# Linear attention into a gated long convolution: k and v dealt to 116 partitions in runs of five tokens, and the last output rows of two batches computed as one tile

## The chip, the cores and the metric

The kernel runs on one core of one Trainium2 chip. The metric is the device time of one execution in microseconds; the number given for a kernel is the median of its runs. A core has a matrix engine (TensorE, PE in the profile; its weight loads are PEld), a vector engine (VectorE, DVE), a scalar engine (ScalarE, ACT), GpSimd (POOL) and a queue engine (SyncE, SP). Each runs its own instructions in order and waits on semaphores. Transfers are issued from SP, ACT and POOL and carried by the core's 16 DMA engines.

## What is computed

Inputs are q, k and v of shape (8 batches, 8 heads, 576 tokens, 64), and three weights. First comes a linear attention, in which phi weights the positive part of a row by cosine and sine of its token's place:

```python
def phi(x, c, s):
    r = np.maximum(x, 0.0)
    return np.concatenate([r * c, r * s], axis=-1)
kv  = einsum('bhsf,bhsd->bhfd', phi(k), v)      # sum over the tokens s
z   = sum over s of phi(k)
att = einsum('bhsf,bhfd->bhsd', phi(q), kv) / (phi(q) . z + 1e-6)
```

The heads side by side make x of shape (8, 576, 512). Then x @ w_proj gives three blocks x1, x2, x3; x2 is convolved along the tokens with a filter, by a Fourier transform of length 576; and the output is (x1 * conv(x2) * x3) @ w_out, of shape (8, 576, 512) in float32.

What matters for the change: the sum over tokens in kv and z does not care which token lies on which partition, so long as k and v agree and the cosine and sine columns fit. The rows of q, and so of the output, do have fixed places.

## The kernel before

**Tokens on partitions.** A batch has 576 = 5 * 115 + 1 tokens. `load_rows` (L156) puts tokens 0 to 511 of four or eight heads on 128 partitions, four successive tokens each (one transfer, runs of 256 elements), and tokens 512 to 575 on partitions 0 to 63 as a fifth column of 64 elements (a second transfer). The unused half of the fifth column, partitions 64 to 127, is filled with zeros by memsets (`step_pad` L234, and L246 for `k32` and `v32`). q, k and v all have this layout. The token numbers are in `s4_i` (L207), from which ACT makes the cosine column `ccol` and the sine column `scol` (L248 and L251); `tcol` and `epsc` come from these.

**Who loads.** The first half of batch 0's k and v comes from SP into the float32 tiles `k32` and `v32` (`step_load32`, words `Sk`, `Sv`). Everything else comes from POOL into six float16 buffers (`step_load`, words `Lq`, `Lk`, `Lv`), cast on the way.

**The steps of a batch.** `pk` (L504 on) makes kp = relu(k) times cosine and sine, 20 instructions a batch on ACT or DVE, through `tsc` (L111) or directly (L514). `va` casts v beside a column of ones (L538, through `ev`, L134 and L138). `kv` (L557) is the sum over tokens: for each of 8 heads five matmuls of 65 columns over all 128 partitions. `pq` makes the products of q, `qt` transposes them (on PE in batches 0 and 1, by a DMA transpose from SP after), `num` multiplies with kv and divides into `att`. `fx` and `pr` go to x2, `dft`, `mul` and `inv` do the convolution, `xt` and `ga`/`gb` the two gates (L736), `g` and `y` their product, and `out` the last matmul.

**The last rows.** The output of a batch comes in four tiles of 128 rows (`out` groups 0 and 1, L824) and the last 64 rows (group 2). For these `y` writes the tile `ye` of 64 columns. `out_tile` (L818) then runs eight matmuls (L829): 64 rows by 256 columns each, the two halves of the 512 columns on the two halves of the PSUM partitions. `left` (L853) evicts 128 x 256 elements on ACT and stores them by two transfers of 64 rows.

**What sets the order.** The order on every engine is written out by hand: the string that `run` (L890) reads. A word such as `pk0.1'a*2` runs two parts of step `pk` of batch 0, half 1, on ACT (`'v` is DVE); each part ends at a `yield`. An engine takes its instructions in this order. PSUM tiles (`unit`, L69) come from a ring of four. Words with `~` are loads that also wait for the last DVE instruction and DMA transpose named before them (`hold`, L148).

Of the kernel before, what the change touches and what calls it, by code (L numbers as in the profile page):

```python
# [17 lines left out]
def kernel(  # L18
# [19 lines left out]
    nc = tc.nc  # L38
# [21 lines left out]
    NM = NC * 128  # L60

# [104 lines left out]

    def step_load(nm):
        def load(b, half):
            raw_t[(b, nm)] = raw_buf[(3 * b + "qkv".index(nm)) % len(raw_buf)]
            load_rows(nc.gpsimd, raw_t[(b, nm)], {"q": q, "k": k, "v": v}[nm], b, at(half))  # L170
            yield
        return load

    def step_load32(nm):
        def load(b, half):
            load_rows(nc.sync, k32 if nm == "k" else v32, k if nm == "k" else v, b, at(half))
            yield
        return load
# [26 lines left out]
    def step_iota(part):  # L205
        if part == 0:
            iota("s4_i", [128, NJ], lambda t: [  # L207
                (t[:, 0:4], [[1, 4]], 0, 4), (t[0:64, 4:5], [[1, 1]], NM, 1),
                (t[64:128, 4:5], [[1, 1]], 0, 1),
            ])  # L210
            yield
            return
# [29 lines left out]
    def step_cols():  # L242
        nc.vector.memset(warm, 0.0)
        nc.vector.memset(half_pi, PI / 2.0)
        for r in (k32, v32):
            nc.vector.memset(r[64:128, :, 4 * D : 5 * D], 0.0)  # L246
        yield
        nc.scalar.activation(  # L248
            out=ccol, in_=cc["s4_i"], func=AF.Sin, scale=-(PI / 2.0) / S, bias=half_pi
        )  # L250
        nc.scalar.activation(out=scol, in_=cc["s4_i"], func=AF.Sin, scale=(PI / 2.0) / S)  # L251
        yield
# [5 lines left out]
        nc.vector.reciprocal(out=epsc, in_=ccol)  # L258
        yield
        nc.vector.tensor_tensor(out=tcol, in0=epsc, in1=scol, op=AL.mult)  # L260
# [244 lines left out]
    def step_pk(b, half):  # L505
# [4 lines left out]
        for j in range(NJ):  # L510
            for x, col in enumerate((ccol, scol)):
                dst, src, c = kp_t[b][:, j, hs, x], rw[:, hs, ds(j * D, D)], col[:, j : j + 1]
                if which[0] == "a":
                    nc.scalar.activation(out=dst, in_=src, func=AF.Relu, scale=c)  # L514
                else:
                    tsc(dst, src, c, AL.mult, 0.0, AL.max)
                yield
# [21 lines left out]
    def step_va(b, x):  # L539
# [3 lines left out]
            va_buf[b % 2][:, hs, :, 0:D],  # L543
            (v32 if b == 0 and x < 2 else raw_t[(b, "v")])[:, hs].rearrange(
# [11 lines left out]
    def step_kv(b, half):  # L556
# [3 lines left out]
        for g in range(hv.start, hv.stop):  # L560
            for h in range(4 * g, 4 * g + 4):
                for j in range(NJ):
                    nc.tensor.matmul(  # L563
                        u[:, g, ds((h % 4) * 65, 65)], kp[:, j, h].rearrange("p a b -> p (a b)"),
                        va[:, h, j, 0:65], start=(j == 0), stop=(j == NJ - 1),
# [220 lines left out]
    def step_y(b, c, n):  # L786
# [24 lines left out]
        if "ye" not in moe[b]:  # L811
            moe[b]["ye"] = late["p"].tile([128, NC, 64], FP16, tag="ye", bufs=2, name=f"ye{b}")
        tt(
            out=moe[b]["ye"][:, c : c + n].rearrange("p c (a t) -> p c a t", t=4),
# [5 lines left out]
    def out_tile(b, t, dst, cs):  # L820
        y = moe[b]["y"]
        for c in cs:
            if t < 4:
# [3 lines left out]
                continue  # L827
            for hf in range(2):
                nc.tensor.matmul(  # L829
                    dst[ds(64 * hf, 64), 0 : DM // 2], moe[b]["ye"][:, c],  # L830
# [22 lines left out]
    def left(b, u):  # L853
        os_ = late["p"].tile([128, DM // 2], FP32, tag="os4", bufs=1, name=f"os{b}_4")
# [35 lines left out]
    def run(plan, **batch):  # L890
# [15 lines left out]
        cols io0 pad1 Sk0.0 pad2 cols io2 rows io1 cols rows th tf warm0.12 cols*5 Sv0.0  # L906
        rows pad0 th'v rows*3 th'v cols*3 rows pk0.0'a*2 rows pk0.0'a*2 tf pk0.0 rows
        pk0.0'a tf pk0.0 cols*2 rows va0.1 cols ones0 rows*2 pk0.0*2 rows va0.0'v pk0.0'a
        th'v Lq0.0 Lq0.1 kv0.0 rows pq0.0 pq0.0'a*4 pq0.0 pq0.1*2 qt0.1 pq0.1*3 Lk0.1 qt0.0
        pq0.1'a qt0.2 kv0.0 qt0.1'b num0.1 tf pk0.1'a pk0.1*3 tf pk0.1 qt0.0'c num0.0 pk0.1  # L910
        ones1 pk0.1'a pk0.1*2 Lv0.1 va0.2 num0.0 num0.1 pk0.1'a va0.3'v qt0.2'b Lw0 kv0.1*2
        num0.1 num0.0 num0.1 cols Lw2 num0.0 qt0.3 rows Lq1.2 num0.2*2 cols*2 xp0.0 qt0.3'b
        rows num0.2 rows num0.2 Lk1.2 xp0.0*2 xp0.0'a num0.3*4 xp0.1 Lv1.2 ga0.0 gb0.3 Lw1
        xp0.1*2 pad4 cols pad5 ti xp0.1'v cols pad3 Lf gb0.0*2 tf ga0.0 gb0.0 ga0.0 Lf
        gb0.3*2 ga0.3 gb0.2 ti tf th ~Lq2.2 cols ~Lk2.2 cols pq1.2*2 pq1.2'a pq1.2*2 pq1.2'a
        rows gb0.2 ga0.3 ga0.1*2 ga0.3'v ti cols fx0.1 fx0.0 pk1.2 gb0.2 pk1.2 gb0.1*2 ga0.1
        fx0.3 fx0.1 pk1.2*2 fx0.0'v ga0.2 pk1.2 fx0.2 th gb0.1 fx0.3 fx0.2 ga0.2*2 pk1.2
        tf'v pk1.2*4 qt1.0 va1.0'v kv1.2 va1.1'v kv1.2 th kv1.2 qt1.1 g0.0.2 qt1.0'v th
        ~Lq3.1 tf qt1.0'v qt1.1'v qt1.2 qt1.1'v qt1.2 ~Lk3.0 qt1.2 num1.0*3 tf pr0.1 th
        num1.1 num1.0 num1.2 g0.2.2 num1.1 tf ~Lq3.0 num1.2 num1.1 pr0.1 tf ti pr0.0 num1.2  # L920
        num1.1 qt1.3 num1.2 pr0.0 pr0.2 qt1.3 dft0.0 feo0 pr0.2 dft0.0 feo1 h0 qt1.3'v xp1.0
        ti xp1.0 pq2.2 fx1.1 pq2.2 h0'v h1 ~Lv2.2 pq2.2 xp1.0 pq2.2 pk2.2 xp1.0'v pk2.2
        pk2.2'a h0 fx1.1 pk2.2 num1.3*3 pq2.2 num1.3 pq2.2 qt2.3 h2 qt2.0 fx1.2 h1 pk2.2 h1
        pk2.2 xp1.1 fx1.3 xp1.1 ~Lk3.1 ~Lq4.1 ~Lv3.1 h2 fx1.2 xp1.1'v fx1.3 xp1.1'v fx1.0
        pk2.2*2 dft0.1 dft0.1'v ~Lo dft0.2 ga1.0 fx1.0 dft0.2 mul0 ti mul0 pr1.0 pr1.2 ti*2
        mul0 ga1.0 mul0 pr1.1 pr1.1'v pr1.0 ga1.0 inv0.1 inv0.0 ~Lq4.0 ti pk2.2 late pr1.2
        dft1.2 dft1.0 dft1.2'v inv0.1 dft1.1 pk2.2 inv0.0 inv0.2 va2.0'v dft1.0 kv2.2 pq3.2
        va2.1'v inv0.3 kv2.2 y0.0.2 ~Lk4.1 y0.0.2 dft1.1 inv0.2 ga1.2*2 mul1 gb1.2 mul1
        qt2.1 kv2.2 num2.0 ~Lv3.0 qt2.2 num2.0 inv0.3 num2.1 pq3.2'a ga1.2 gb1.2 ~Lv4.0
        num2.1 num2.0 num2.1 num2.0 num2.1 gb1.3*2 mul1*2 gb1.2 gb1.1*2 pq3.2'a pq3.2 gb1.3  # L930
        pq3.2'a ga1.1 pk3.2 gb1.1 num2.2 ~Lk4.0 num2.2*3 y0.0.2 ga1.1 y0.0.2 fx2.1 y0.2.2
        ga1.1 y0.2.2 gb1.0*2 pk3.2'a fx2.1 inv1.1 fx2.2 pk3.2 gb1.0 inv1.1 fx2.2 ga1.3
        y0.2.2 ga1.3 inv1.0 inv1.0'v ga1.3 xp2.0 num2.3*3 xp2.0*3 num2.3 pk3.2 inv1.3*2
        y0.0.2 inv1.2*2 fx2.0*2 fx2.3*2 g1.0.2 ga2.0 xp2.1*2 pr2.0 xp2.1*2 pq3.2 ga2.0
        y0.2.2 qt3.0 va3.0'v y1.0.2 pk3.2 pk3.2'a*2 pk3.2 y0.2.2 pk3.2'a pq4.2 pr2.1 ga2.0
        qt3.2 pq4.2 out0.0 pr2.2 pr2.1 pr2.0 out0.0 dft2.1 y1.0.2 dft2.0 ~Lq5.0 va3.1'v
        y1.0.2 ~Lq5.1 ~Lv4.1 y1.0.2 pk3.2 ~Lv5.0 qt3.1 y1.2.2*2 pr2.2'v dft2.1 y1.2.2 dft2.2
        kv3.2*2 y1.0.2 gb2.1 y0.2.2 gb2.1 dft2.0 g1.2.2 y0.0.2 pq4.2'a ~Lv5.1 qt3.3 dft2.2'v
        kv3.2 gb2.0*2 mul2*2 num3.0*4 ~Lk5.0 gb2.1 gb2.0 gb2.3 pk4.2'a gb2.3*2 ~Lk5.1 out0.2
        ga2.2*2 fx3.0 out0.2 pq4.2'a ga2.1 mul2*2 ga2.2 fx3.0 num3.1*2 num3.2*2 pk4.2'a  # L940
        ga2.1 num3.1 pk4.2 out0.1 num3.2 num3.1 y1.2.2 ga2.1 num3.2 num3.3*2 pk4.2 pk4.2'a
        num3.3*2 ga2.3 gb2.2 ga2.3 xt3 pq4.2'a gb2.2 out0.1 fx3.1 fx3.2 ga2.3 inv2.1 gb2.2
        fx3.3 pq4.2 qt4.0 qt4.1 pk4.2'a pk4.2*2 fx3.3 fx3.1'v fx3.2'v inv2.1 pk4.2'a inv2.0
        pk4.2 inv2.0 g2.2.2 qt4.2 va4.0'v va4.1'v y2.0.2*2 pr3.0*2 pr3.1 pq5.2 pr3.1 kv4.2
        g2.0.2 y1.2.2 ~Lk6.0 ~Lq6.0 kv4.2*2 pq5.2'a pr3.2 ga3.0 pk5.2 pr3.2'v pk5.2 y1.2.2
        ga3.0 inv2.2 out0.2 dft3.2 ~Lk6.1 inv2.2'v dft3.0*2 dft3.2'v dft3.1*2 num4.0 inv2.3
        pk5.2*2 inv2.3 num4.0 y1.0.2 pq5.2'a gb3.1 num4.1 num4.0*2 num4.2 mul3 gb3.1 num4.1
        ~Lq6.1 pq5.2'a out1.0*2 num4.2 num4.1 pq5.2'a qt4.3 num4.1 ga3.1*2 pq5.2'a y2.0.2
        num4.2 gb3.0 num4.2 y2.0.2 y2.2.2 num4.3 gb3.0 num4.3 out0.0 out1.1*2 y2.2.2 num4.3
        gb3.3 fx4.0 qt5.2 num4.3 fx4.2 gb3.2 mul3 xt4 gb3.3'v ga3.2 qt5.1 mul3 pk5.2 fx4.0  # L950
        fx4.2 mul3 fx4.1 g3.0.2 inv3.0 qt5.0 gb3.2 qt5.3 fx4.3 y2.2.2 ga3.2 fx4.1 pk5.2*3
        inv3.0'v fx4.3 pk5.2 inv3.1 inv3.1'v y2.2.2 y3.0.2*2 pk5.2'a pr4.0 y3.0.2 inv3.3
        pr4.0 y2.2.2 inv3.3 out1.2*2 pr4.2 out1.2 pr4.1 y3.0.2 ~Lq7.0 va5.0'v kv5.2 y2.0.2
        va5.1'v pr4.1'v inv3.2 pq6.2 pr4.2 kv5.2 ga4.0 pk6.2*2 ~Lv6.1 ga4.0'v inv3.2 kv5.2
        out0.1 dft4.2 pq6.2 pq6.2'a*2 pq6.2 dft4.1 dft4.0 ga3.3 dft4.2 dft4.0'v pk6.2 dft4.1
        mul4 ~Lq7.1 num5.0*3 ga3.3 ~Lv6.0 num5.0 ~Lk7.1 gb4.1 num5.1*2 g3.2.2 pk6.2'a*2
        out2.0 gb4.1 y3.2.2 out1.0 out2.0 pk6.2'a pk6.2 pk6.2'a gb4.0 num5.1 gb4.0 num5.1
# [61 lines left out]
```

## Time and profile before

| | us |
|---|---|
| median of 3 runs (222.70 to 224.93) | 223.49 |
| the profiled execution | 224.69 |
| its span | 222.9 |
| PE busy | 207.7 |
| DVE busy | 194.7 |
| ACT busy | 170.7 |
| POOL busy | 65.5 |

How to read what follows. Busy time is given per engine over the span; the chain of work is what ended last, followed backwards. A line of the timeline has start and length in us, engine, line of the kernel, operation, output tile <- input tiles, shape, and in brackets how long the engine had been idle and what ended that. A line of the groups has the count after the shape, then total busy time and mean ns of one, then idle time ahead of them. `SPq` is an issue on SP's queue: its length is the time of issuing, not of the transfer. Queue q0 carries what POOL issues, q1 what SP issues. The profile lists for the first loads from SP 3.9 us (k) and 5.9 us (v) from issue to landing, and medians of 6.9, 7.2 and 6.5 us for the half loads of q, k and v from POOL.

### The profile page before, as it was taken

To read this page: it belongs to the slowest core of one execution; us is meant where nothing else is said; L and a number is where in the kernel's file an instruction comes from. 1 tells how busy PE (TensorE), PEld (TensorE's weight loads), DVE (VectorE), ACT (ScalarE), POOL (GpSimd) and SP (SyncE) were. 2 spreads that over 40 slices of the span, in tenths; PEclk is the share of its full clock that TensorE was granted. 3 is DMA by queue.
4 is the path that set the end of the run, shared out by engine and by line. 5 is a ranking of instruction groups with operands and counts; after the bars stand their busy time and mean duration, and the time that the engine had idled before them with its cause. 6 is when DMAs were issued, how large, how long until landed. Compare 5 with 4: busy or idle time off the path is not lost.

```text
span 222.9 us, 5869 instructions
## 1 busy us (share of the span) xinstructions
PE 207.7 (93%) x2316; PEld 142.8 (64%) x2316; DVE 194.7 (87%) x473; ACT 170.7 (77%) x275; POOL 65.5 (29%) x105
## 2 busy tenths in 40 slices
PE   7388989999999999999999999799999999999990
PEld 2176776574888476756686667476876667477630
DVE  7998999989999989989999997889888797589930
ACT  4796989998898999888784975877787736476651
POOL 8892456213962096003500184002200000000000
PEclk9979999999999999999999999999999999999996
DMA  5999999999999999999999999997999940823084
GB/s 170 190 186 192 191 209 193 175 138 210 144 189 184 173 161 182 169 195 163 170 157 194 200 199 182 146 300 156 110 177 149 326 132 3 197 94 138 22 258 165
DMA packets 90907, 38.39 MB, mean 172 GB/s; under 512 B 58944, under 2 KB 86592, under 8 KB 90880
## 3 DMA queue, kind: packets, MB, share of 16 engines
q0 software_dynamic: 38944, 16.26, 59.8%
q1 hardware_dynamic: 51568, 21.17, 46.0%
q10 hardware_dynamic: 368, 0.59, 0.7%
q8 instruction: 18, 0.29, 0.5%
q14 instruction: 9, 0.07, 0.1%
HBM read 33.69 MB, written 9.44 MB: 193 GB/s over the span
## 4 chain that ended last, share of the span: by engine, by line
PE 67%; DVE 14%; DMA 10%; ACT 3%; issue 2%; POOL 2%; ACTq 0%; DVEq 0%; POOLq 0%
PE x L736 22%; PE x L680 11%; PE out L824 10%; DMA xt<-att 4%; PE kv L563 4%; PE num L606 4%; PE dft L711 3%; PE fx L634 3%; DMA out_dram<-os 3%; DMA raw<-in_q_dram 3%; PE inv L770 3%; PE inv L774 2%; DVE kp L111 2%; DVE yf L116 2%; DVE qp L111 2%
## 5 line engine op out<-in xcount | busy, mean ns | idle before, releaser
L736 PE MATMUL x<-xt,wp 128*128 128x288 f16 x512 | 71.2, 286 | 0.6 <-DMA xt<-att 0.3
L736 PEld LDWEIGHTS <-wp 128*128 128x128 f16 x512 | 47.9, 98 | 15.8 <-issue 2.8
L680 PE MATMUL x<-wp,fx 128*128 128x512 f16 (+1 forms) x160 | 34.6, 381 | 0.0
L824 PE MATMUL out<-wo,y 128*128 128x512 f16 x128 | 30.1, 379 | 0.0
L138 ACT ACTIVATE os<-out 128x1024 f32<-128x1024 f32 (+2 forms) x24 | 18.3, 767 | 12.5 <-PE out L824 10.1
L116 DVE TENSOR_TENSOR att<-num,rcp 128x640 f16<-128x640 f32 x32 | 26.0, 819 | 0.6
L680 PEld LDWEIGHTS <-fx 128*128 128x128 f16 (+1 forms) x160 | 13.6, 100 | 15.0 <-issue 2.1
L138 ACT CAST x0s<-x 128x576 f16<-128x576 f32 x27 | 17.2, 641 | 6.0 <-PE x L736 5.1
L138 ACT CAST x2s<-x 128x576 f16<-128x576 f32 x28 | 17.8, 639 | 4.8 <-PE x L736 4.7
L138 ACT ACTIVATE x2f<-x 128x1024 f16<-128x1024 f32 (+1 forms) x18 | 16.2, 903 | 6.6 <-PE x L680 5.6
L158 POOL DMA_DIRECT2D raw<-in_q_dram x14 | 11.2, 797 | 31.4 <-ACT x0s L138 18.2
L824 PEld LDWEIGHTS <-y 128*128 128x128 f16 x128 | 12.1, 98 | 12.6 <-issue 0.4
L138 ACT CAST fx<-fx 128x576 f16<-128x576 f32 x29 | 17.8, 648 | 1.8 <-PE fx L640 1.5
L138 ACT CAST eq<-inv 128x576 f16<-128x576 f32 x26 | 16.0, 648 | 3.9 <-PE inv L774 3.3
L158 POOL DMA_DIRECT2D raw<-in_k_dram x13 | 10.5, 811 | 27.0 <-DVE rcp L617 14.6
L770 PE MATMUL inv<-itab,yf 128*128 128x144 f16 x128 | 16.9, 226 | 1.2 <-ACT x2f L138 0.9
L158 POOL DMA_DIRECT2D raw<-in_v_dram x13 | 10.5, 805 | 21.8 <-DVE rcp L116 17.3
L774 PE MATMUL inv<-itl,yf 128*128 128x288 f16 x64 | 16.8, 286 | 0.0
L563 PE MATMUL kv<-va,kp 128*128 128x65 f16 x320 | 12.4, 193 | 4.0 <-DVE va L134 3.8
L563 PEld LDWEIGHTS <-kp 128*128 128x128 f16 x320 | 11.6, 98 | 5.8 <-ACT kp L514 4.0
L606 PEld LDWEIGHTS <-qpt 128*128 128x128 f16 x320 | 13.0, 98 | 3.6 <-issue 0.9
L606 PE MATMUL num<-kvs,qpt 128*128 128x65 f16 x320 | 14.3, 194 | 0.9 <-ACT qpt L138 0.5
(163 smaller groups left out, 432.8 us busy)
## 6 DMA issues: line engine op xcount, KB each, us to landing
out_dram<-os SPq DMA_DIRECT2D x30, 256.0 KB, 3.2
raw<-in_q_dram POOLq DMA_DIRECT2D x12, 256.0 KB, 6.9
raw<-in_k_dram POOLq DMA_DIRECT2D x11, 256.0 KB, 7.2
raw<-in_v_dram POOLq DMA_DIRECT2D x11, 256.0 KB, 6.5
wp<-in_moe_w_proj_dram POOLq DMA_DIRECT2D x3, 512.0 KB, 8.6
raw<-in_q_dram POOLq DMA_DIRECT2D x2, 512.0 KB, 12.1
raw<-in_k_dram POOLq DMA_DIRECT2D x2, 512.0 KB, 13.3
raw<-in_v_dram POOLq DMA_DIRECT2D x2, 512.0 KB, 10.5
```

Of the source, the lines that this page charges most:

```text
L111: last_dve[0] = nc.vector.tensor_scalar(out=out, in0=in0, scalar1=s1, scalar2=s2, op0=op0, **({"op1": op1} if op1 else {}))
L116: last_dve[0] = nc.vector.tensor_tensor(out=out, in0=in0, in1=in1, op=op)
L138: return nc.scalar.copy(out=out, in_=in_) if mul is None else nc.scalar.mul(out=out, in_=in_, mul=mul)
L158: first = queue.dma_start(out=rw[:, to, 0 : 4 * D], in_=src[b, hs, 0:NM].rearrange("h (p j) d -> p h (j d)", j=4),)
L563: nc.tensor.matmul(u[:, g, ds((h % 4) * 65, 65)], kp[:, j, h].rearrange("p a b -> p (a b)"), va[:, h, j, 0:65], start=(j == 0), stop=(j == ...
L606: nc.tensor.matmul(u[:, hh, ds(t * 65, 65)], qpt_buf[:, h, ds(t * 128, 128)], kvs[:, h // 4, ds((h % 4) * 65, 65)], start=True, stop=True,)
L634: nc.tensor.matmul(uf[:, ds(256 * t, 144)], att[:, c, t], fm.rearrange("p v a -> p (v a)"), start=(t % 2 == 0), stop=False,)
L680: nc.tensor.matmul(dst, fx[:, c, ds(128 * ch, n)], wp16[:, c, ds(DM, DM)], start=(c == cs[0]), stop=(c == cs[-1]),)
L736: nc.tensor.matmul(u[:, hf, 0:HS], wp16[:, i, ds(w * DM + c * 128, 128)], xt[:, i, ds(HS * hf, HS)], start=(i == 0), stop=(i == NC - 1),)
L770: nc.tensor.matmul(u[:, comp, ds(par * QS, QS)], yf[:, comp, ds(par * DM + c * 128, 128)], itab[:, par + 4 * comp], start=(par == 0), stop ...
L774: nc.tensor.matmul(u[:, comp, 0:HS], yf[:, comp, 2 * DM : NF], itl[:, c, comp].rearrange("p a b -> p (a b)"), start=False, stop=True,)
L824: nc.tensor.matmul(dst, y[:, c, ds(QS * t, 128)], wo16[:, c], start=(c == 0), stop=(c == NC - 1),)
```

## The change

k and v get a layout of their own. Partition p holds tokens 5p to 5p + 4, for p from 0 to 115; partition 115 has one valid token (575), its other four places hold what follows in memory, that is the next head's first tokens. One transfer with runs of 320 elements loads a half (four heads) or a whole batch. Only the very last half, at the end of the input, takes two: 115 partitions, and one token. The kv matmuls read 116 partitions for column 0 and 115 for columns 1 to 4, so the extra places never enter. `kp` and `va` are made on 116 partitions. The zero filling stays for q's buffers alone (`pad0`, `pad3`). `ccol` and `scol` now follow a new iota `k_i` with 5p + j; `tcol` and `epsc` are made from two further columns in the old order, `cq` and `sq`. q keeps `load_rows`.

For batches 0 to 5 the last 64 rows of two batches are computed together: `ye` holds both, four matmuls of 128 x 512 replace two times eight, one eviction of 128 x 512 replaces two of 128 x 256, and two stores of 64 rows x 512 replace four. Batches 6 and 7 stay as they were.

```diff
+    BP = B - 2
+    KP = S // NJ + 1
+    KJ = (KP,) + (KP - 1,) * (NJ - 1)
...
+    def load_runs(queue, rw, src, b, hs):
+        to = slice(0, rw.shape[1]) if rw.shape[1] < NH else hs
+        rows = src[b, hs].rearrange("h s d -> h (s d)")
+        last = b == B - 1 and hs.stop == NH
+        n = KP - 1 if last else KP
+        runs = bass.AP(
+            tensor=rows.tensor, offset=rows.offset, ap=((NJ * D, n), rows.ap[0], (1, NJ * D))
+        )
+        hold(queue.dma_start(out=rw[0:n, to], in_=runs))
+        if last:
+            queue.dma_start(
+                out=rw[n:KP, to, 0:D], in_=rows[:, (S - 1) * D :].unsqueeze(0)
+            )
...
-            load_rows(nc.gpsimd, raw_t[(b, nm)], {"q": q, "k": k, "v": v}[nm], b, at(half))
+            (load_rows if nm == "q" else load_runs)(nc.gpsimd, raw_t[(b, nm)], {"q": q, "k": k, "v": v}[nm], b, at(half))
...
-            load_rows(nc.sync, k32 if nm == "k" else v32, k if nm == "k" else v, b, at(half))
+            load_runs(nc.sync, k32 if nm == "k" else v32, k if nm == "k" else v, b, at(half))
...
+            iota("k_i", [128, NJ], lambda t: [(t, [[1, NJ]], 0, NJ)])
...
-        for r in (k32, v32):
-            nc.vector.memset(r[64:128, :, 4 * D : 5 * D], 0.0)
         yield
-        nc.scalar.activation(
-            out=ccol, in_=cc["s4_i"], func=AF.Sin, scale=-(PI / 2.0) / S, bias=half_pi
-        )
-        nc.scalar.activation(out=scol, in_=cc["s4_i"], func=AF.Sin, scale=(PI / 2.0) / S)
-        yield
+        cq, sq = small("cq", NJ), small("sq", NJ)
+        for n, co, si in ((cc["k_i"], ccol, scol), (cc["s4_i"], cq, sq)):
+            nc.scalar.activation(out=co, in_=n, func=AF.Sin, scale=-(PI / 2.0) / S, bias=half_pi)
+            nc.scalar.activation(out=si, in_=n, func=AF.Sin, scale=(PI / 2.0) / S)
+            yield
...
-                        u[:, g, ds((h % 4) * 65, 65)], kp[:, j, h].rearrange("p a b -> p (a b)"),
-                        va[:, h, j, 0:65], start=(j == 0), stop=(j == NJ - 1),
+                        u[:, g, ds((h % 4) * 65, 65)], kp[0 : KJ[j], j, h].rearrange("p a b -> p (a b)"),
+                        va[0 : KJ[j], h, j, 0:65], start=(j == 0), stop=(j == NJ - 1),
...
+            if b < BP:
+                nc.tensor.matmul(
+                    dst, moe[b]["ye"][:, c].rearrange("p b n -> p (b n)"), wo16[:, c],
+                    start=(c == 0), stop=(c == NC - 1),
+                )
+                continue
...
+        if b < BP:
+            ev(os_, u[:, 0], OUTSC)
+            yield
+            for x in range(2):
+                nc.sync.dma_start(out=out[b - 1 + x, NM:S], in_=os_[ds(64 * x, 64)])
+            yield
+            return
```

In the order string, the words `pad1`, `pad2`, `pad4`, `pad5` and the separate `out` groups 2 of batches 0 to 5 go; `out1.2*3`, `out3.2*3` and `out5.2*3` (matmuls, eviction and stores in one piece) stand right after the last part of `y1.0`, `y3.0` and `y5.0`. The third of them comes in here, with the eviction of x2's first block (`pr7.0`) ahead of it and that of the second (the second `pr7.1`) behind:

```
before: pr7.0 pr7.1 inv6.2 pr7.0 out5.1'v y4.0.2 y5.0.2 y6.0.2*4 pr7.2 out4.2 pr7.1 dft7.1
after:  pr7.0 pr7.1 inv6.2 pr7.0 out5.1'v y4.0.2 y5.0.2 out5.2*3 y6.0.2*4 pr7.2 pr7.1 dft7.1
```

The first word now is the iota (`io0`), which came after the first memsets before. All other words keep their order.

## Prediction

> **What bounds the kernel now.** I read the whole page first, then busy time by stretches, then the timeline of the start, then the chain of work that ended last. From the page, busy time by engine and the DMA queues:
>
> ```profile
> PE 207.7 (93%) x2316; PEld 142.8 (64%) x2316; DVE 194.7 (87%) x473; ACT 170.7 (77%) x275; POOL 65.5 (29%) x105
> ...
> q0 software_dynamic: 38944, 16.26, 59.8%
> q1 hardware_dynamic: 51568, 21.17, 46.0%
> ```
>
> PE is idle for 222.9 - 207.7 = 15.2 us. The two DMA queues together hold the 16 engines for 106% of the span, so packets of both overlap: the DMA engines have little slack. Where PE and DVE idle is told by stretch (columns: stretch, its length, busy time of PE, PEld, DVE, ACT, POOL, PE clock, DMA share, GB/s):
>
> ```profile
> 5.00:10.00 5.00, 1.77 (x13) 0.73 (x12) 4.72 (x31) 3.53 (x9) 4.20 (x7) 1.00 1.37 208
> 10.00:15.00 5.00, 4.53 (x63) 4.03 (x60) 4.56 (x18) 4.61 (x10) 5.00 (x7) 0.66 1.42 182
> 15.00:20.00 5.00, 3.77 (x77) 3.19 (x74) 4.45 (x20) 4.17 (x8) 2.43 (x4) 1.00 1.28 196
> 20.00:25.00 5.00, 4.68 (x40) 3.31 (x38) 4.46 (x16) 3.69 (x10) 0.66 (x2) 1.00 1.59 186
> 25.00:30.00 5.00, 5.00 (x54) 4.27 (x52) 5.00 (x15) 5.00 (x9) 3.03 (x4) 1.00 1.47 199
> ```
>
> PE waits at the start; DVE, the engine that feeds it, has only 0.44 + 0.55 + 0.54 = 1.5 us of holes from 10 to 25 us and none after. In later stretches DVE is busy 9.96 of 10 us (30 to 40), 9.42 (40 to 50), 9.90 (50 to 60), and PE 20.00 of 20 from 100 to 120 and from 160 to 180. So what the start loses, no later stage gives back. The start itself, from the timeline (start, length, engine, line):
>
> ```profile
> 0.74 0.46 SPq L158 DMA_DIRECT2D k<-in_k_dram  x1
> 1.26 0.75 SPq L163 DMA_DIRECT2D k<-in_k_dram  x1
> 2.06 0.60 SPq L158 DMA_DIRECT2D v<-in_v_dram  x1
> 2.70 0.63 SPq L163 DMA_DIRECT2D v<-in_v_dram  x1
> ...
> 4.71 0.51 ACT L514 ACTIVATE kp<-k,ccol 128x256 f16<-128x256 f32 x1 [1.78 <-DMA k<-in_k_dram]
> ...
> 9.19 0.48 DVE L134 CAST va<-v 128x640 f16<-128x640 f32 x1
> ...
> 9.72 0.80 PE L563 MATMUL kv<-va,kp 128*128 128x65 f16 x20 [3.23 <-DVE va L134]
> ```
>
> The first work of ACT waits for the k load (landed 3.9 us after issue), the first real matmul for v's cast; v's load has landed at about 8.0 (2.06 + 5.9), 1.2 us before DVE reads it. This stretch carries the case.
>
> **What the Trainium skill says.** "DMA: Bandwidth & Descriptors", section "Why a DMA increments its semaphore by 16 and not by 1": the number of engines of a transfer is the largest k up to 16 that divides the slowest dimension of both sides; 100 partitions get 10 engines and 127 get 1; from the SP and ACT queues it is the lowest-numbered k. It adds that transfers issued from GpSimd sometimes get 16 engines instead, with the partitions dealt out in shares rounded up. The trace of before can't confirm this: its transfers have 128, 96 or 64 partitions, all multiples of 16. 116 is 4 x 29, so the rule gives 4; 115 gives 5. "TensorEngine Tiling (Array Packing)", section "Key Properties": tiles of the array work independently and in parallel. Here the trace agrees: the 8 matmuls of a last-rows tile at L829, 0.27 us each, take 0.56 us together, two by two.
>
> **Part 1: k and v on SP, for batch 0.** Prices are the trace's packet records: on the SP queue 18 ns for 256 B, 46 ns for 1024 B, 85 ns for 2048 B, so by interpolation 56 ns for 1280 B, the new run of five tokens. Before, one load was 512 x 46 + 256 x 18 ns = 28.2 us of engine time, 1.8 us on 16 engines. After it is 464 (116 x 4 heads) x 56 ns = 26.0 us: 1.6 us on 16 engines, 6.5 us on 4. I take 4: the rule is stated for exactly this queue, and nothing in the trace speaks against it. The bound on the other side is 15 or 16 engines (rival one).
> With 4: packets begin at about 2.0 us as now. k would be done at 8.5, v behind it on the same four engines at 15.0, if nobody shared. But q's loads from POOL, on all 16, begin at 6.2 us by the packet records and continue beyond 20 us. When two queues met there (6.5 to 7.0) the 16 engines did 10.3 us of packet time in 8 us, so each of two queues gets some 0.65 of an engine. k's remaining 2.3 us then end at 9.7, v's 6.5 us at 19.7. I take the middle for v: 17.4, visible at 17.6 (k's packets ended some 0.2 us ahead of its reader). Cast 0.48 and its step to PE 0.05 put the first kv matmul at 18.2 instead of 9.72: +8.5 us, bounds 15.0 and 19.7, that is +6.1 and +10.8.
> Queued behind the waiting cast on DVE are all of batch 0's q products, the second half of k and the att products; behind it on ACT the casts of qpt; PE waits for both. SP issues its next transfer only in batch 2, POOL's queue is not blocked, so the later loads run ahead: the waits of DVE between 10 and 25 us (1.5 us) shrink. I give back 1.0. Net of part 1: +7.5 us.
>
> **Part 2: k and v from POOL.** Here q0's records say 60 ns for 1024 B cast to 512 B, 32 ns for 256 B cast to 128 B; by the same slope 70 ns for 1280 B cast to 640 B. A half load falls from 512 x 60 + 256 x 32 = 38.9 to 464 x 70 = 32.5 us of engine time, with 304 packets fewer: over 30 half loads 0.19 ms / 16 = 12 us per engine, against 236 us of both queues. If GpSimd's exception holds, the busiest engine has 8 partitions: 32 x 70 ns = 2.24 us instead of 2.43. The loads are read long after they land, so this is worth 0 on the path; it could give up to 1.4 us where PE waits for the slow transpose of xt (PE 9.55 of 11 us between 136 and 147). POOL issues 0.7 us less per half load: hidden, it is 29% busy. Without the exception each half load takes 32.5 / 4 = 8.1 us: rival two.
>
> **Part 3: less filling with zeros.** Eight memsets of 0.27 us become two. The four at 1.3 to 2.4 us gain nothing: the next DVE work (sgn, 2.43) needs POOL's sg_i, made at 2.23 to 2.39, and POOL now makes one iota more (0.15). Two of the three near 21 to 23 us go: -0.5 us. The two added ACT sines (0.30 and 0.19 us) lie in ACT's 1.78 us wait for k: 0. Cover gone, 0.5.
> 116 partitions instead of 128 change no length: time goes by columns.
>
> **Part 4: last rows of two batches together.** Removed are six groups of L829 on PE; added are three groups of four matmuls with 512 columns, at the 1.73 us per 8 of L824: 0.87 each.
>
> ```profile
> L138 ACT ACTIVATE os<-out 128x256 f32<-128x256 f32 x7 | 2.7, 386 | 0.0
> L138 ACT ACTIVATE os<-out 128x512 f32<-128x512 f32 x4 | 2.4, 597 | 2.6 <-PE out L824 2.4 <-DMA out_dram<-os 0.3
> L829 PE MATMUL out<-wo,ye 128*64 128x256 f16 x64 | 5.0, 278 | 0.0
> ```
>
> First two pairs: 4 x 0.56 removed, 2 x 0.87 added: -0.5 us of PE. ACT: 6 x 0.39 removed, 3 x 0.60 added, off the path. Of output transfers SP issues six fewer. The third pair is put between the second x2 block of batch 7 and its eviction: the new tile ends at about 195.4 + 0.87 = 196.3, its eviction (0.60) stands ahead of x2f's on ACT (1.02, now at 195.19), so dft starts at about 197.9 instead of 196.64: +1.2; the 0.56 removed at 202.25 leaves +0.6. Sum of part 4: +0.1.
>
> **Sum.** 7.5 + 0 - 0.5 + 0.1 = +7.1 us. Against the profiled execution: 222.9 + 7.1 = 230.0 span, and 1.8 us around it (224.69 - 222.9) make 231.8. The median of the runs is 1.2 us below that execution, so 223.5 + 7.1 = 230.6.
>
> **Rivals.** One, not slower: SP's transfers spread over 15 or 16 engines after all. Then v is even issued at 1.26 instead of 2.06 and lands earlier; DVE, which reads it at 9.19, is not waiting for it, so the gain is parts 2 to 4, 0 to -1.5: 222.7. The point that decides is the engine count: both loads are 52 us of engine time and must fit in the 7 us between 2.0 and 9.0, which takes about 8 engines. For it: only a rule I cannot see here speaks against it. 28%.
> Two, slower still: POOL's k and v also sit on four engines. Batch 1's k load (full, 13.3 us to land now, issued 13.0, read at 27.3) has 1.0 us to spare and would take 16.2 us of packets alone; with part 1's delay of 7.5 partly covering it, about 5 us more: 236. 24%.
>
> **Chances.** Forecast (SP on 4 engines, POOL spread) 48%, own range 227.5 to 234; rival one 28%, 221 to 224.5; rival two 24%, 232 to 241. The range 221 to 237 leaves out half of rival two's upper part and a little of rival one. About 1% is what a measurement of this kernel can tell from no change. Faster by over 1% (under 221.3): a quarter of rival one and some of the xt gain, 0.10. Within 1%: most of rival one and the forecast's edge, 0.19. Slower: 0.71.
>
> **What would show it.** k and v of batch 0: issue to landing 9 us and 14 to 18 us instead of 3.9 and 5.9; first kv matmul near 18; no idle DVE from then to 25; six L829 groups gone and os 128x512 x7. It is wrong if k lands within 5 us of issue (rival one), or if POOL's k and v take over 12 us to land while q's stay near 7 (rival two).

## The result and the profile after

The changed kernel takes 318.15 us (median of 4 runs, 317.43 to 319.84) against 223.09 us for the kernel before on the same chip (4 runs, 222.22 to 224.93): 1.4256 times as long, 95% interval 1.4146 to 1.4367. That is 95 us more, where the prediction said 7.1 and its range ended 13.5 above the median before. The profiled span is 315.9 us, 93.0 more. Here and below a median is over all runs of a kernel, while ratios and their intervals leave out the runs that lie more than 1.5% above its fastest, so that the two differ where the runs of a kernel spread.

First the page of the kernel after: busy time by engine, the two queues, and the transfers with their KB and median us from issue to landing.

```profile
PE 224.9 (71%) x2280; PEld 149.3 (47%) x2280; DVE 198.9 (63%) x467; ACT 171.8 (54%) x274; POOL 67.9 (21%) x82
...
q0 software_dynamic: 70464, 16.48, 51.0%
q1 hardware_dynamic: 50424, 21.18, 45.8%
...
raw<-in_q_dram POOLq DMA_DIRECT2D x12, 256.0 KB, 11.7
raw<-in_k_dram POOLq DMA_DIRECT2D x10, 290.0 KB, 15.1
raw<-in_v_dram POOLq DMA_DIRECT2D x10, 290.0 KB, 12.2
```

PE is now idle for 315.9 - 224.9 = 91.0 us, before 15.2. The other 17.2 us of the 93.0 are PE's own: it is busy longer with 36 matmuls fewer, at a lower clock (mean granted clock 0.877, before 0.983). The clock is low in the holes and right after them: 0.62 to 0.82 in the five stretches of 10 us from 130 to 180 us, in which PE is busy 1.5 to 8.6 us, and 1.00 from 180 to 230 us, where it is busy 7.2 to 10.0. q0 moves about as many bytes as before (16.48 against 16.26 MB) in 70,464 packets instead of 38,944, though the change should have saved 304 packets a half load. And the half loads of k and v take 15.1 and 12.2 us to land (7.2 and 6.5 before); q's, which the change does not touch, 11.7 (6.9).

The stretches of the start (stretch, length, busy time of PE, PEld, DVE, ACT, POOL, PE clock, DMA share, GB/s):

```profile
5.00:10.00 5.00, 1.32 (x4) 0.30 (x2) 2.35 (x13) 0.00 (x0) 5.00 (x6) 0.94 1.26 157
10.00:15.00 5.00, 0.00 (x0) 0.10 (x1) 1.95 (x14) 2.10 (x5) 0.91 (x2) 0.50 1.17 131
15.00:20.00 5.00, 0.00 (x0) 0.00 (x0) 0.00 (x0) 0.00 (x0) 1.54 (x3) 0.50 1.25 211
20.00:25.00 5.00, 0.04 (x2) 0.04 (x2) 0.59 (x2) 0.59 (x1) 3.65 (x2) 0.50 1.13 151
25.00:30.00 5.00, 4.63 (x51) 4.09 (x51) 3.37 (x16) 4.64 (x11) 0.79 (x1) 0.51 1.36 135
```

and the timeline that explains them:

```profile
0.74 0.38 SPq L178 DMA_DIRECT2D k<-in_k_dram  x1
1.18 0.86 SPq L178 DMA_DIRECT2D v<-in_v_dram  x1
...
11.54 0.51 ACT L530 ACTIVATE kp<-k,ccol 116x256 f16<-116x256 f32 x1 [8.33 <-DMA k<-in_k_dram]
...
24.41 0.49 DVE L137 CAST va<-v 116x640 f16<-116x640 f32 x1 [10.94 <-DMA v<-in_v_dram]
...
24.96 0.38 PE L579 MATMUL kv<-va,kp 116*128 116x65 f16 x4 [18.64 <-DVE va L137]
```

k is read 10.8 us after its issue, v 23.2 us after; the first kv matmul stands at 24.96 (9.72 before). No engine but POOL does anything between 15 and 20 us, and PE's clock is 0.50. "TensorE: Matmul & The Clock Gate", section "Part 1: The HAM clock gate (the 'warmup' mystery)", of the Trainium skill says that an idle array gets half its clock until it has been busy for a while; this trace agrees, 0.50 and still 0.51 from 25 to 30 us while PE is busy, then 1.00 from 30 to 40 us.

The start loses 15 us; the rest is elsewhere. The chain that ended last (start, length, what), its DMA pieces alone:

```profile
7.61 23.06 DMA raw<-in_v_dram
...
42.62 20.71 DMA raw<-in_k_dram
...
69.04 10.71 DMA qpt<-qp
...
81.89 9.99 DMA raw<-in_q_dram
91.89 10.22 DMA raw<-in_v_dram
...
122.07 28.69 DMA raw<-in_k_dram
...
158.86 12.51 DMA qpt<-qp
...
203.22 11.33 DMA xt<-att
...
228.58 13.40 DMA qpt<-qp
```

With the two pieces left out here (5.75 and 4.38) they make 150.8 us, 48% of the span. 82.7 us are loads of k and v by POOL (23.06 + 20.71 + 10.22 + 28.69), 36.6 are transposes of q. The change does not touch these, but their median time to landing went from 3.8 to 10.4 us. So three things must be told apart: SP's two loads, POOL's loads, and the last rows, which the prediction priced at +7.5, 0 and +0.1.

### The profile page after: what moved, and what is told of

The parts are those of the page before. It is cut to its first block, busy times and chain, and to the rows that moved or that the text cites. A ratio compares the mean times of both kernels' runs of the same rounds, so it can differ in the third digit from the quotient of the medians.

```text
span 315.9 us, 5737 instructions
## 1 busy us (share of the span) xinstructions
PE 224.9 (71%) x2280; PEld 149.3 (47%) x2280; DVE 198.9 (63%) x467; ACT 171.8 (54%) x274; POOL 67.9 (21%) x82
## 3 DMA queue, kind: packets, MB, share of 16 engines
q0 software_dynamic: 70464, 16.48, 51.0%
## 4 chain that ended last, share of the span: by engine, by line
DMA 48%; PE 31%; DVE 10%; POOL 4%; issue 3%; ACT 2%; SPq 0%; DVEq 0%; POOLq 0%; ACTq 0%
DMA raw<-in_k_dram 16%; DMA qpt<-qp 12%; DMA raw<-in_v_dram 11%; PE x L752 10%; DMA xt<-att 5%; PE out L845 5%; PE x L696 4%; DMA raw<-in_q_dram 3%; POOL raw L178 2%; PE num L622 2%; PE inv L786 1%; PE kv L579 1%; DVE qp L114 1%; PE inv L790 1%; DMA out_dram<-os 1%
## 5 line engine op out<-in xcount | busy, mean ns | idle before, releaser
L752 PE MATMUL x<-xt,wp 128*128 128x288 f16 x512 | 76.4, 300 | 15.0 <-DMA xt<-att 13.7
L752 PEld LDWEIGHTS <-wp 128*128 128x128 f16 x512 | 50.5, 102 | 33.1 <-DMA xt<-att 14.9
L845 PE MATMUL out<-wo,y 128*128 128x512 f16 x128 | 32.0, 395 | 0.5 <-DVE y L119 0.5
L622 PE MATMUL num<-kvs,qpt 128*128 128x65 f16 x320 | 15.5, 201 | 23.5 <-DMA qpt<-qp 18.7
L178 POOL DMA_DIRECT2D raw<-in_k_dram x13 | 20.5, 1581 | 51.6 <-DVE ye L119 29.1
L141 ACT CAST x0s<-x 128x576 f16<-128x576 f32 x27 | 17.2, 642 | 24.8 <-PE x L752 24.1
L114 DVE TENSOR_SCALAR kp<-raw,ccol 116x512 f16<-116x512 f16 (+1 forms) x29 | 12.2, 420 | 26.6 <-DMA raw<-in_k_dram 26.6
L178 POOL DMA_DIRECT2D raw<-in_v_dram x13 | 19.9, 1536 | 35.2 <-DVE ye L119 21.2
L579 PE MATMUL kv<-va,kp 115*128 115x65 f16 (+1 forms) x320 | 12.9, 196 | 20.3 <-DVE va L137 19.3
L161 POOL DMA_DIRECT2D raw<-in_q_dram x14 | 11.2, 799 | 65.5 <-DVE va L137 26.2
L119 DVE TENSOR_TENSOR rcp<-num,epsc 128x10 f32<-128x10 f32 x32 | 5.1, 165 | 31.1 <-PE num L622 30.6
L579 PEld LDWEIGHTS <-kp 115*128 115x128 f16 (+1 forms) x320 | 12.0, 100 | 22.3 <-issue 13.0
L696 PEld LDWEIGHTS <-fx 128*128 128x128 f16 (+1 forms) x160 | 13.3, 100 | 16.3 <-issue 2.9
L141 ACT CAST xf<-dft 128x1024 f16<-128x1024 f32 (+1 forms) x16 | 13.6, 901 | 12.0 <-PE dft L727 11.6
## 6 DMA issues: line engine op xcount, KB each, us to landing
raw<-in_q_dram POOLq DMA_DIRECT2D x12, 256.0 KB, 11.7
raw<-in_k_dram POOLq DMA_DIRECT2D x10, 290.0 KB, 15.1
raw<-in_v_dram POOLq DMA_DIRECT2D x10, 290.0 KB, 12.2
```

The lines of the kernel that those rows point to most:

```text
L114: last_dve[0] = nc.vector.tensor_scalar(out=out, in0=in0, scalar1=s1, scalar2=s2, op0=op0, **({"op1": op1} if op1 else {}))
L119: last_dve[0] = nc.vector.tensor_tensor(out=out, in0=in0, in1=in1, op=op)
L141: return nc.scalar.copy(out=out, in_=in_) if mul is None else nc.scalar.mul(out=out, in_=in_, mul=mul)
L161: first = queue.dma_start(out=rw[:, to, 0 : 4 * D], in_=src[b, hs, 0:NM].rearrange("h (p j) d -> p h (j d)", j=4),)
L178: hold(queue.dma_start(out=rw[0:n, to], in_=runs))
L579: nc.tensor.matmul(u[:, g, ds((h % 4) * 65, 65)], kp[0 : KJ[j], j, h].rearrange("p a b -> p (a b)"), va[0 : KJ[j], h, j, 0:65], start=(j = ...
```

## Experiments on the loads

Theory: every transfer of 116 partitions, SP's and POOL's, runs on four DMA engines, and POOL's are most of the loss. Rivals: SP's late v alone sets everything back; or the merged rows do.

Where a load is cut, `load_runs` issues it as two transfers, of 112 partitions and the rest, because 112 = 16 x 7:

```diff
-        hold(queue.dma_start(out=rw[0:n, to], in_=runs))
+        for lo, hi in ((0, 112), (112, n)) if CUT else ((0, n),):
+            runs = ...  # rows lo to hi
+            load = queue.dma_start(out=rw[lo:hi, to], in_=runs)
+            if lo == 0: hold(load)
```

**E1, E2, E3.** The change, with `CUT` for SP's two loads only (E1), for POOL's only (E2), for all (E3).

> Only SP's two loads of batch 0 are cut into 112 partitions (16 x 7) and 4; POOL's k and v keep 116. Theory one (a transfer is spread only over as many engines as divide its partitions, on both queues, and most of the loss is POOL's): k lands in about 4 us instead of 10.7, v in about 6 instead of 23, the first kv matmul comes near 10 instead of 25, and the time falls by 8 to 15 us only, to 303 to 311. Theory two (the late start is the loss, and the later waits follow from it): 222 to 235. Theory three (the merged last rows or the new order of words are the loss): within 5 us of 318.

> Only POOL's k and v loads are cut into 112 partitions and 4; SP's two loads keep 116. Theory one: half loads land in 6 to 8 us again, the 4-byte packets of POOL's queue fall from 42,016 to some 3,000, and what is left is the late start: 230 to 238, where the prediction put it. Theory two (late start is the loss): over 300. Theory three (last rows or order): over 300.

> All k and v loads are cut into 112 partitions and 4; layout, order and merged last rows stay. Theory one: the whole loss goes, 220 to 226, with one short packet-poor transfer more per load. Theory three: stays over 300.

E1 took 312.34 us (309.26 to 316.18), ratio 1.393 [1.3864, 1.3996]; E2 266.67 (265.78 to 269.27), 1.1952 [1.1899, 1.2005]; E3 251.87 (249.5 to 254.43), 1.1222 [1.1172, 1.1272]. The cut of POOL's loads gives back 51.5 us, that of SP's only 5.8 while POOL's are whole and 14.8 when they are not. With all of them cut, 28.6 us over the kernel before remain that no load explains.

**E8, E10, E12.** The loads alone: last rows and their order as before. All loads whole (E8), SP's whole and POOL's cut (E10), all cut (E12).

> Loads of k and v to 116 partitions in one transfer, as in the change; last rows and their order as before. If the losses add up: 318 less the 28 of the merged rows, 285 to 296. If the two share the same waits (slow transposes behind both): 300 to 316.

> Last rows as before, POOL's loads cut 112 and 4; only SP's two loads go to 116 partitions in one transfer. This measures part 1 of the prediction alone, which said +7.5 (bounds 5.1 to 9.8): 229 to 233. From the pair of earlier runs that differ in just this (266.7 and 251.9), 14.8: 238.

> Runs of five tokens with every load cut into 112 and 4 partitions, last rows and their order as before: the loads' part of the change on sixteen engines. Prediction's rival one said 0 to -1.5 for parts 2 to 4, of which parts 2 and 3 are here: 222 to 224. If there is a gain in fewer packets or fewer memsets, below 222.5.

E8: 289.5 us (285.29 to 292.38), ratio 1.2821 [1.275, 1.2893]. E10: 237.47 (237.11 to 237.7), 1.0612 [1.0552, 1.0673]. E12: 222.78 (222.39 to 223.79, 22 runs), 0.9971 [0.9955, 0.9987], which beats both kernels, by a little. So SP's two loads cost 237.5 - 222.8 = 14.7 us, and POOL's add 289.5 - 237.5 = 52.0 (49 by the two lower of E8's four runs). On 16 engines the new layout is worth -0.7 us against its own runs of before. The transfers of E12, from its page, are as quick as those of before:

```profile
raw<-in_k_dram POOLq DMA_DIRECT2D x11, 280.0 KB, 6.2
raw<-in_v_dram POOLq DMA_DIRECT2D x11, 280.0 KB, 6.2
raw<-in_q_dram POOLq DMA_DIRECT2D x12, 256.0 KB, 6.9
```

and in E10 all that is lost is one wait at the start (engine, line, what it waited for: us in total, times, longest):

```profile
PE kv L583 <- DVE va L137: 18.9, 2, 18.5
...
ACT va L141 <- DMA v<-in_v_dram: 9.9, 1, 9.9
```

**E14.** POOL's loads whole, SP's cut, last rows as before: do POOL's cost so much by themselves?

> SP's two loads in pieces of 112 and 4 partitions, POOL's k and v in one of 116, last rows as before. If the costs of the parts add up, POOL's loads by themselves take 52 to 60 us: 275 to 283 us. If they cost only together with SP's two at the start: under 250.

279.43 us (278.95 to 284.85), ratio 1.2497 [1.2403, 1.2591]: 56.6 us above E12. They do. Its chain has pieces of the same kind:

```profile
13.57 20.74 DMA raw<-in_k_dram
...
51.25 20.56 DMA raw<-in_v_dram
...
115.39 31.64 DMA raw<-in_k_dram
```

The first two are loads of a whole batch, which took 13.3 us (k) and 10.5 us (v) before. The third is a half load, the last of seven that POOL issues in one row (median before 7.2 us). The landings of all half loads, from the page of E14:

```profile
raw<-in_k_dram POOLq DMA_DIRECT2D x10, 290.0 KB, 13.3
raw<-in_v_dram POOLq DMA_DIRECT2D x10, 290.0 KB, 12.0
```

**How many engines, and what stands on the idle ones.** The packet records answer this by counting. Before, q0 has 1,376 packets of 4 bytes: 86 transfers x 16. After, it has 42,016. Take 4 working engines for 116 partitions and 5 for 115, and one 4-byte packet on each idle engine for each data packet on a working one: a half load has 464 data packets, 116 on each of four engines, so 12 x 116 = 1,392. With 28 half loads of 116, two of 115 (11 x 92 each), two of a single token (12 each), and 16 for each of the queue's 62 transfers as before, the sum is 38,976 + 2,024 + 24 + 992 = 42,016, to the packet. In E12 the same count (112 on 16 engines) gives 2,880, and 2,880 is there. That these packets fill the idle engines is my reading; the numbers are the records'. Their median length is 9 ns, the mean 13.

Two runs vary the number of partitions in POOL's first piece, SP cut, last rows as before: `((0, 104), (104, n))` in E9, `((0, 114), (114, n))` in E15.

> Runs of five tokens, last rows as before, SP's loads cut 112 and 4, POOL's k and v cut into 104 (8 x 13) and 12 partitions: eight engines where the change had four and the 112 cut has sixteen. Theory one with the largest divisor: the 4-byte packets of POOL's queue come to about 14,000 (42,016 with four engines), a half load takes 416 x 69 ns / 8 = 3.6 us of packets, and the time lies between the 224 of sixteen engines and the 275 that four engines on POOL alone would give: 226 to 245. If dealing in rounded-up shares happens for 104: few 4-byte packets and 223 to 225.

> As the last, but POOL's loads in pieces of 114 and 2 partitions: 114 is 6 times 19, so six engines by the count, with 10 times 76 four-byte packets for a half load. If the time follows the number of working engines (16: 222.8, 13: 226.8, 4: about 278), six take 240 to 262 us; if one transfer over fewer than 16 engines costs the same whatever their number, 270 or more.

E9: 226.79 us (223.34 to 233.46, 12 runs), ratio 1.0066 [1.0025, 1.0108] (from runs with a median of 225.4). Its 4,800 packets of 4 bytes fit 13 engines (104 = 8 x 13), not the eight that I expected by an arithmetic slip: 13 is the largest divisor up to 16. E15: 262.07 us (256.94 to 266.46); its 25,824 packets fit six engines. The runs of E15, E13 and E4 spread over 4 to 10 us, so no interval is given for these three.

| engines of POOL's main piece | 16 (E12) | 13 (E9) | 6 (E15) | 4 (E14) |
|---|---|---|---|---|
| time, us | 222.8 | 226.8 | 262.1 | 279.4 |
| 4-byte packets on q0 | 2,880 | 4,800 | 25,824 | 42,016 |
| data packets of the main piece on one engine (448, 416, 456, 464 x 69 ns / engines), us | 1.9 | 2.2 | 5.2 | 8.0 |

**E11, E13.** Is it the 4-byte packets, or the data bunched on few engines? Both add to E12 one transfer after each POOL load, into a tile that nothing reads: 113 single elements (E11), or the first four elements of every run (E13).

```diff
+        if queue is nc.gpsimd:   # E13; E11: one partition, 113 runs of 1
+            queue.dma_start(out=fill[0:n, :, 0:4], in_=<the same rows, ap=((NJ * D, n), rows.ap[0], (1, 4))>)
```

> As the run with all loads cut 112 and 4 and last rows as before, but behind each POOL load of k and v goes one transfer of 113 single elements to one partition of a scratch tile that nobody reads: 113 is prime, so one engine carries data and, by theory one, the other fifteen get 113 packets of 4 bytes each, some 47,000 in all, without the data being bunched. If the 4-byte packets are what costs: over 250. If bunching the data on four engines is what costs: 223 to 230, the rest being POOL's 28 further issues.

> Every k and v load in two pieces of 112 and 4 partitions, last rows as before, and after each POOL load one more transfer into a tile that nothing reads: 112 or 116 partitions of the same rows, but only four elements of each, so 464 packets of 8 B for a half load instead of 1280 B. By the count of the 116-partition loads it should go over four engines with 116 four-byte packets on each of the twelve others, some 36,000 in all, with next to no data. If these filler packets make POOL's 52 us: 265 to 280 us. If the data bunched on four engines does: no more than the 113 single elements of the run before cost, 230 to 242 us, with xt landing after 8 to 12 us.

E11 missed its aim: its 113 data packets brought only 15 of 4 bytes with each transfer. The packet records show why: the packets of data come mostly in groups of eight, 3 to 4 ns apart, and 16 x 8 - 113 = 15. So this transfer was dealt to all 16 engines in shares rounded up, which is what the prediction called GpSimd's exception. It cost 13.3 us all the same: 236.11 us (235.07 to 238.1), ratio 1.0568 [1.0503, 1.0633], with POOL busy 78.5 us instead of 63.3, 15.2 more.

E13 made 42,272 packets of 4 bytes, about as many as E14, with 3.6 KB a transfer instead of 290. It took 262.42 us (258.27 to 262.98), 39.6 above E12. But it does not bring back what E14 shows, since its half loads land as quickly as those of E12:

```profile
raw<-in_k_dram POOLq DMA_DIRECT2D x11, 280.0 KB, 6.1
raw<-in_v_dram POOLq DMA_DIRECT2D x11, 280.0 KB, 5.8
```

What E13 adds is issuing. POOL is busy 104.8 us, 41.5 more than in E12 (the fills of k take 1.55 us each). In both runs the loss is close to what POOL issues more, 13.3 us for 15.2 and 39.6 for 41.5, while E14 has only 5.4 us more of it (68.7) and loses 56.6. So issuing can explain E11 and E13, but not E14; and 4-byte packets in the same number, without the data, did not make the loads land late. What part they have in E13's loss stays open. What is left for E14 is the data bunched on few engines, as the table suggests. No run shows that alone, for a load on few engines always brought both.

## Experiments on the last rows

**E4, E5, E6, E7.** Theory: the merged tile itself is cheap, but its store, issued in one piece with matmuls and eviction, stands in SP's queue ahead of transposes and waits for an eviction that comes late. Rival: the longer eviction and the later matmuls on ACT and PE. E4 is the kernel before with only the merged last rows, in the change's places. E5 issues their stores later. E6 puts them where before had the last rows of the second batch of each pair. E7 is E6 with all loads of the change, cut.

```diff
E4:  y1.0.2 out1.2*3 pq5.2'a
...
-E5: qt4.3 num4.1
+E5: y1.0.2 out1.2*2 pq5.2'a
...
+E5: qt4.3 out1.2 num4.1
-E6: inv3.3 pr4.2 pr4.1
+E6: inv3.3 out1.2*2 pr4.2 out1.2 pr4.1
```

The other two tiles of E5 have their stores behind `qt6.3` and `xt7`; in E6 all words `out1.2`, `out3.2` and `out5.2` stand where before has words of that name.

> The kernel before with only the merged last rows and their places in the order. Theory one: 0 to +1 us on before (prediction's part 4 said +0.1): 222 to 225. Theory three: most of the loss shows here, over 250.

> As the run with the merged last rows alone (251), but the three stores of merged rows are issued later on SP: behind the last qpt transpose of batch 4, that of batch 6, and the xt transpose of batch 7. Matmuls and evictions stay where they were. Theory four (SP's queue: the store waits for its eviction and holds the transposes behind it): 223 to 230, and PE's waits for qpt and xt go. Theory five (the matmul placed right behind the last part of y: PE waits for ye, and ACT for PE): stays at 243 to 252.

> The merged last rows, with matmuls, eviction and store of a pair in the three places of the order string where the second batch of the pair had them before. Loads as before. Theories four and five alike: no added wait, some 0.3 us of PE less per pair, 221.5 to 224.

> Runs of five tokens for k and v with every load cut into 112 and 4 partitions, and the merged last rows in the old places. Theories one and four together: nothing is left of the loss, 220.5 to 224, and if the fewer packets are worth anything it is below the run with merged rows in the old places alone. If the layout itself costs (116 partitions, order of sines): above 226.

E4: 251.17 us (246.02 to 255.0), 27.9 above the median before; its lowest run is 22.8 above. E5: 232.49 (231.36 to 233.73), ratio 1.0407 [1.037, 1.0443]. E6: 224.97 (224.25 to 225.52), 1.0058 [1.0031, 1.0085]. E7: 224.75 (224.06 to 225.09), 1.0054 [1.0033, 1.0074]. The queue of SP shows it, first in the kernel before,

```profile
95.36 4.63 SPq L577 DMA_TRANSPOSE qpt<-qp  x3
100.10 2.09 SPq L858 DMA_DIRECT2D out_dram<-os  x2
102.28 1.36 SPq L577 DMA_TRANSPOSE qpt<-qp  x1
```

then in E4:

```profile
96.43 4.63 SPq L578 DMA_TRANSPOSE qpt<-qp  x3
105.91 1.19 SPq L871 DMA_DIRECT2D out_dram<-os  x2
107.20 3.12 SPq L578 DMA_TRANSPOSE qpt<-qp  x1
```

In both a store stands between the third and the fourth transpose of q. Before, it is that of `out0.2`, whose eviction is long done; now it is the merged one, and SP stands still from 101.1 to 105.9. The transpose behind it starts 4.9 us later than before (1.1 of that was lost ahead of the store). At the other end PE waits, which it did not before; the first line is before, the second E4:

```profile
108.50 0.47 PE L606 MATMUL num<-kvs,qpt 128*128 128x65 f16 x10
...
118.07 0.73 PE L607 MATMUL num<-kvs,qpt 128*128 128x65 f16 x10 [7.59 <-DMA qpt<-qp]
```

These matmuls come 9.6 us later, twice what the transpose lost at its start, because it also takes longer. It lands 10.8 us after its issue, before within 6.2. Before, it was issued ahead of POOL's next half loads; now it comes after them:

```profile
103.69 0.75 POOL L158 DMA_DIRECT2D raw<-in_k_dram  x1 [14.20 <-DVE rcp L617]
...
104.77 0.75 POOL L159 DMA_DIRECT2D raw<-in_k_dram  x1 [14.24 <-ACT xf L139]
```

By the packet records the packets of 256 bytes on SP's queue pass at up to 806 per us while it runs before, at no more than 284 in E4. So the wait in the queue also moved the transpose into other traffic.

SP waits longest for the third store, 16.1 us. The transpose of xt behind it, before and in E4:

```profile
188.22 3.17 SPq L660 DMA_TRANSPOSE xt<-att  x1
...
213.58 1.13 SPq L871 DMA_DIRECT2D out_dram<-os  x2
214.81 3.72 SPq L661 DMA_TRANSPOSE xt<-att  x1
```

SP's waits for the evictions of last rows sum it up, for the kernel before and for E4:

```profile
SPq L858 <- ACT os L138: 7.7, 2, 4.0
```

```profile
SPq L871 <- ACT os L139: 30.6, 3, 16.1
```

Moving only the stores (E5) gives back 18.7 of 27.9 us, moving the tiles as well (E6) 26.2. Of E5's remaining 9 us the chain shows one new step,

```profile
106.86 6.15 DMA out_dram<-os
```

for which ACT waits 2.2 us with the eviction of the next output tile; PE also waits for the last part of y right ahead of the merged matmuls (3.0 us). E6 removes both; which weighs more was not tried. E6 and E7 stay 1.3 and 1.2 us slower than before, although PE is busy 206.8 us in E6 against 207.7. This is not explained. E7 is all of the change but for whole loads and the places of the rows, so all that the rest of it costs, on balance, is these 1.2 of the 95 us.

## Why the prediction was wrong

The sum of the parts, along the runs: E12 - before = 222.8 - 223.1 = -0.3; SP's loads 14.7 (E10 - E12); POOL's 52.0 (E8 - E10); merged rows 28.7 (after - E8). Together they make 95.1, but formed in this way they must add up. That the last two hold in other company as well is what counts: POOL's whole loads cost 51.5 to 60.5 in four pairs of runs, the merged rows 27.9 to 32.9 in five. SP's loads do not: 14.7 and 14.8 where POOL's are cut, 5.8 (the change against E1) and 10.1 (E8 against E14) where they are whole.

**What bounds the kernel: right, and used too little.** "What the start loses, no later stage gives back" held: E10 loses 14.7 us. But the page said in the same place that the two queues hold the 16 engines for 106% of the span. A kernel so loaded has no room for transfers that sit on a quarter of the engines (56.6 us in E14), and the prediction drew that conclusion for the start only.

**Part 1, SP's loads, +7.5: mechanism right, size half.** They do run on four engines. Packets of 1280 B took 55 ns (I had 56), and the four engines were full with some 75 of them per us before q began. The term that failed is v at 17.6. "Each of two queues gets some 0.65 of an engine" is what was wrong: from 7 us on, beside q's packets, SP's came at 28 to 50 per us, 37 on average, x 55 ns = 2.0 us of packets per us on four engines, 0.5 of each. The page "DMA: Bandwidth & Descriptors", section "Queues, rings and completion order", of the Trainium skill says that each engine goes round-robin between its queues, packet by packet, which agrees and would have given it: v's 6.4 us of packets at half speed take 12.8 and end near 24. Even the upper bound of 19.7 was too low. The give-back of 1.0 did not show.

**Part 2, POOL's loads, 0: the step that failed.** POOL's loads on four engines cost 52.0 to 56.6 us where the sum had 0. I took "GpSimd's exception" to hold. The rule of divisors ("DMA: Bandwidth & Descriptors", section "Why a DMA increments its semaphore by 16 and not by 1", of the Trainium skill), which the page states for both kinds of queue, holds for POOL too: the counts fit 4, 5, 6, 13 and 16 engines for 116, 115, 114, 104 and 112 partitions. The exception, stated for some transfers only, did not occur in any load of k or v, only in E11's small transfers. POOL's k and v on four engines had a name and 24%: rival two. Its engine time was right (8.1 us a half load; 464 x 69 ns / 4 = 8.0), its price of 5 us was not; E14 - E12 gives 56.6. It was taken from the slack of one load, batch 1's k. "The loads are read long after they land" was true of before; but every batch brings such loads, each takes twice as long to land, and other transfers are delayed with them: in E14, where nothing else is changed against E12, q's half loads land in 9.7 us instead of 6.9, the transposes of q in 6.1 instead of 3.8. (In the change it is 11.7 and 10.4, with the merged rows on top.) A transfer that slows all others must be priced against every reader, not against its own. Also "304 packets fewer" was right for data packets and left out the 4-byte ones, and "POOL issues 0.7 us less per half load" did not come: the one transfer takes 1.58 (k) and 1.54 us (v) to issue, the two of before 1.60 and 1.47 together, on average.

**Part 3, zeros, -0.5: consistent.** E12 contains parts 1 to 3 on 16 engines and gains 0.7. The split between fewer zeros and the rest was not tried. That 116 partitions change no length held: kp takes 0.51 us as before, the cast of v 0.49 against 0.48. Rival one foresaw 222.7 with all loads on 16 engines and the merged rows; E3 comes nearest to that, and took 251.9. That E12 took 222.78 without the merged rows does not bear it out.

**Part 4, merged rows, +0.1: the second step that failed.** On ACT it was priced as it went, on PE nearly so. The groups by shape after the change are

```profile
L141 ACT ACTIVATE os<-out 128x512 f32<-128x512 f32 x7 | 4.1, 596 | 9.2 <-PE out L850 5.8 <-DMA out_dram<-os 2.9 <-PE out L845 0.5
...
L850 PE MATMUL out<-wo,ye 128*128 128x512 f16 x12 | 3.5, 416 | 2.4 <-DVE ye L119 2.4
```

The evictions are seven of 0.60 us, as foretold; the 12 matmuls take 3.5 us where 2.6 were foretold (3.1 in E6). But "of output transfers SP issues six fewer" counted the transfers and did not ask what they wait for and what is queued behind them on SP. Moving the stores alone gives back 18.7 of the 27.9 us, moving the tiles with them 26.2.

**Direction.** Slower was right. Of the sign named for rival two, POOL's k and v over 12 us to land appeared; q's near 7 did not, since they rose as well, which is the very cost that its price left out.

## What to carry to other kernels

Before changing a transfer's partition count, find its largest divisor up to 16, and keep the bulk on a multiple of 16 with the remainder as a second transfer: 112 + 4 took 222.8 us where 116 took 289.5. Price a slow transfer against all that shares its engines, not against the slack of its own reader. In an in-order queue, look behind each store that is moved or merged: what it waits for, everything behind it waits for too (three stores, E4 against E5: 18.7 us).

## What was not expected of the hardware

POOL's transfers come with 4-byte packets whose numbers fit one rule in all runs counted here: besides 16 per transfer, each engine gets as many packets as the fullest, and what it lacks in data is made up with packets of 4 bytes. That makes 42,016 after against 1,376 before, 558 us of packet time in all against 24, and E11's 15. E13's transfers of 3.6 KB took POOL as long to issue (1.55 us) as the loads of 290 KB in the changed kernel (1.58); the two pieces of E12 take 0.67 each. The issue does not follow the bytes.
